# A delta-rule attention with two expert layers: state copies split by PSUM bank, the last output stored by token groups

## The chip, the core and the metric

The kernel runs on one core of a Trainium2 chip. Its engines are TensorE (PE in the profile, with its weight loads as PEld), VectorE (DVE), ScalarE (ACT), GpSimd (POOL) and the DMA queues, which SP and ACT issue to. The metric is the device time of one execution in microseconds; 3 runs give a median.

## What is computed

Three stages follow each other. The first is a delta-rule recurrence over 768 time steps for 4 batches and 8 heads of width 48; the other two are dense layers over the 3072 tokens that it gives, 384 to 2048 to 384.

```python
for t in range(S):                                    # S = 768
    y[:, :, t] = einsum('bhd,bhde->bhe', q[:, :, t], state)
    v_old = einsum('bhde,bhd->bhe', state, k_n[:, :, t])
    state = state + beta_t * einsum('bhd,bhe->bhde', k_n[:, :, t], v_t - v_old)
x = y.transpose(0, 2, 1, 3).reshape(3072, 384)
h = x @ w_in;  x = (h * tanh(softplus(h))) @ w_out            # first layer
h = x @ w2_in; out = (h * clip(h + 3, 0, 6) / 6) @ w2_out     # second layer
```

## The kernel before

The recurrence is computed in 24 chunks of 32 time steps; the four batches lie beside each other on the 128 partitions, 32 each. Each chunk t takes its inner inverse, multiplies the state into its keys (`ksps`), makes its updates `u`, and adds their outer products to the state. The state is the SBUF tile `sbd`. For chunks 0 to 3 the sum over the chunks stays in PSUM, in two banks `dps[0]` and `dps[1]` (in the profile `dsps`): the bank b // 2 holds batch b, on partitions from 64 (b % 2) (`S_part`, line 791). After each of these chunks' matmuls (`S_mm`, L818) `S_copy` (line 795) copies the four batches to `sbd`, two copies a batch: the even batches by DVE (L804), the odd ones by ACT (L801). The next chunk's `ksps` matmuls (L767) need all of them. From chunk 4 on `S_add` (L829) adds on DVE.

The first layer's tokens come in blocks of 512 (6 blocks, each four chunks); it starts as soon as chunk 3's tokens are there, at about 96 us, and runs beside the rest of the recurrence. The second layer starts at about 657 us and runs alone. Each block n of it has 16 steps: `hps` matmuls (L1127), two activations, and 12 matmuls that add to four accumulators `p` (L1285), one for each group s of 128 rows: partition 32 b + t and group s are time step 32 s + t of the block, of batch b. `flush2` (line 1291) copies the four accumulators to the tile `osb`, in turn by ACT (L1300) and DVE (L1298), and then stores the block batch by batch (L1305): a store is 32 rows x 4 groups x 384 numbers, 192 KB. In the last block two of the four stores are issued by ACT, the others by SP.

Nothing is scheduled at run time but the waits. The order of the instructions on each engine is made while the kernel is built, by the class `Flow` (line 28): each part of the work is a generator that asks for an engine and a time, and `Flow` picks the earliest by fixed costs. `warm` (line 1438) fills TensorE with matmuls of no use until the first layer's first step. Two instructions on different engines that read the same PSUM bank get a wait between them.

Of the kernel before, what the change touches and what calls it, by code (L numbers as in the profile page):

```python
# [8 lines left out]
F32 = mybir.dt.float32  # L9
# [3 lines left out]
ACTF = mybir.ActivationFunctionType  # L13
# [3 lines left out]
C = 32  # L17
# [109 lines left out]
def tile_delta_rule__moe_mish__moe_hardswish(  # L127
# [12 lines left out]
    nc = tc.nc  # L140
    B, H, S, D = q.shape
    NT, DM = out.shape
# [8 lines left out]
    NB = NS // 4  # L151
# [12 lines left out]
    flow = Flow()  # L164

    with tc.manual_schedule():
# [18 lines left out]
        sbd = ap_.tile([128, B, NP, 2 * D], F32, name="sbd")  # L185
# [20 lines left out]
        def room(*keys):  # L206

            first = keys[0][0] in "KUS"  # L210

            def test():
                x = sorted((bank_at[b], b) for b in usable if bank_at[b] is not None)
                others = len(keys) + sum(k[0] != "H" for k in held)
                fits = len(x) >= len(keys) + (0 if first else sum(chain))
                if len(usable) < 8 and keys[0][0] != "H" and others >= len(usable):
                    fits = False
                if first:
                    chain[:] = [] if fits or len(usable) == 8 else [len(keys)]
                if not fits:  # L220
                    return None
                x = x[:len(keys)]
                for key, (_, b) in zip(keys, x):
                    bank_at[b], held[key] = None, b
                return x[-1][0]
            return test
# [5 lines left out]
        def release(key):  # L232
            bank_at[held.pop(key)] = flow.cur
# [557 lines left out]
        def S_part(b, r):  # L791

            return dps[b // 2][64 * (b % 2):64 * (b % 2) + D, r]

        def S_copy(t, b):

            for r in range(2):
                o = sbd[64 * r:64 * r + D, b, :, D * r:D * (r + 1)]
                if b % 2:
                    yield "ACT", 0.33, 0  # L800
                    nc.scalar.activation(out=o, in_=S_part(b, r), func=ACTF.Copy)  # L801
                else:
                    yield "DVE", 0.35, 0
                    nc.vector.tensor_copy(out=o, in_=S_part(b, r))  # L804
            if t == 3 and b % 2:
                release(("S", b // 2))
            flow.set(f"sbd{t}.{b}")

        def S_mm(t):

            if t == 0 or t >= 4:
                for half in range(2):
                    dps[half] = bank(("S", half), [128, 2, NP, D], "dsps")
            for r in range(2):
                for j in range(NP):
                    for b in range(B):
                        p = slice(C * b, C * (b + 1))
                        nc.tensor.matmul(  # L818
                            out=S_part(b, r)[:, j, :],
                            lhsT=kp(t)[p, j, r, 0:D], rhs=ut[t][p, 2 * j + r, :],  # L820
                            start=(t == 0 or t >= 4) and j == r == 0, stop=True, skip_group_check=True,
                        )
            flow.set(f"S{t}")
# [10 lines left out]
        def rec():  # L834


            for t in range(NS):
# [8 lines left out]
                if t:  # L846
# [18 lines left out]
                    if tg:  # L865
# [4 lines left out]
                    r = ap_.tile([128, H, D], F32, tag="r", name="r")  # L870
                    nc.vector.tensor_tensor(
                        out=r.rearrange("p h d -> p (h d)"), in0=vt.pop(t).rearrange("p h d -> p (h d)"),
# [4 lines left out]
                else:  # L877
                    r = vt.pop(t)
# [28 lines left out]
                if 0 < t < 4:  # L907
                    u = gp.tile([128, 512], F32, tag="ghi", name="u")[:, 0:H * D].rearrange("p (h d) -> p h d", h=H)
                else:
                    u = ap_.tile([128, H, D], F32, tag="u", name="u")  # L910
# [6 lines left out]
                if t < 4:  # L917
                    if t == 0:
                        yield room(("S", 0), ("S", 1))
                    yield "PE", 0.8, None, 64  # L920
                    S_mm(t)
                    flow.add(mu(t), pen=0.02)
                    for b in range(B):
                        flow.add(S_copy(t, b))
                    continue
                yield f"mt{t}"
                if not last:
# [15 lines left out]
        def mu(t):  # L943
            yield f"mt{t}"
            yield "PE", 0.85, None, 64
            MU_pe(t)
            yield from finish_y(t)
# [148 lines left out]
        xhl, acc = {}, {}  # L1096
# [104 lines left out]
        def moe():  # L1201
# [34 lines left out]
            while done < 2 * NB * KF - 1:  # L1236
                done += 1
                yield from mm2_second(done)
# [31 lines left out]
        def mm2_second(u):  # L1270
            n, f = divmod(u, KF)
            g, e = divmod(f, 4)
            yield f"lo2.{7 * g + KD + e}"
            yield f"g{u}"
            if f == 0:
                yield f"flush{n - 1}"
            yield "PE", 12 * 0.178, 0
            if f == 0:
                acc[n] = [(ps_o if s < 3 else ps_b).tile([128, DM], F32, tag=f"o{s}", name=f"p{s}") for s in range(4)]
            hi, lo = gs.pop(u)  # L1280
            wh, wl = wo[2, g]
            for s in range(4):
                c = slice(128 * s, 128 * (s + 1))
                for x, (a, w) in enumerate(((hi, wh), (hi, wl), (lo, wh))):
                    nc.tensor.matmul(out=acc[n][s], lhsT=a[:, c], rhs=w[:, e, :],  # L1285
                                     start=(f == 0 and x == 0), stop=(f == KF - 1 and x == 2))
            flow.set(f"mm2.{u}")
            if f == KF - 1:
                flow.add(flush2(n), pen=-0.2)

        def flush2(n):
            a, i = acc.pop(n), n - NB
            yield "lo2.27"
            o = p2.tile([128, 4, DM], F32, tag=f"r{i % 3}", name="osb")
            for s in range(4):
                yield ("DVE", 0.45) if s % 2 else ("ACT", 0.5)
                if s % 2:
                    nc.vector.tensor_copy(out=o[:, s, :], in_=a[s])  # L1298
                else:
                    nc.scalar.activation(out=o[:, s, :], in_=a[s], func=ACTF.Copy)  # L1300
            flow.set(f"flush{n}")
            yield "SP", 0.3
            for b in range(B):
                r0 = b * S + 128 * i
                (nc.scalar if i == NB - 1 and b % 2 else nc.sync).dma_start(  # L1305
                    out=out[r0:r0 + 128, :].rearrange("(t s) d -> s t d", s=C),
                    in_=o[C * b:C * (b + 1)],
                )
            if i == NB - 1:
                flow.set("end")  # L1310

        def phase2():

# [30 lines left out]
        p2 = ps_b = None  # L1344
# [112 lines left out]
        flow.add(matrices(), pen=lambda: 0.0 if "D0" not in flow.ev else 0.3)  # L1457
        flow.add(quads(0), pen=-0.1)
        flow.add(rec(), margin=busy(0.0, 0.8))
        flow.add(scale_v(), pen=busy(0.6, 0.0))  # L1460
        flow.add(loads_start())
# [51 lines left out]
```

## Time and profile before

| | us |
|---|---|
| median of 3 runs | 1069.98 |
| lowest, highest | 1068.26, 1071.07 |
| the profiled execution | 1064.65 |
| its span in the profile | 1062.9 |
| TensorE busy | 1030.7 |
| DVE, ACT, POOL busy | 644.8, 453.5, 224.0 |

The profiled execution is one run of the same program; the times in the rows below count from the start of its span. A row of the instructions in order gives start and duration, and in brackets how long the engine had been idle and which instruction released it; "issue" stands where the profile shows nothing that was waited for. q1 is SP's DMA queue and q10 ACT's. TensorE's granted clock is given as a share of its higher level.

### The profile page before, as it was taken

How to read it: one execution, taken by the hardware profiler on the slowest of the kernel's cores; microseconds unless marked ns; L12 is line 12 of the kernel's file. 1: busy time of each engine (PE TensorE's matmuls, PEld its weight loads, DVE VectorE, ACT ScalarE, POOL GpSimd, SP SyncE). 2: the span in 40 equal slices, each digit the busy share in tenths (PEclk: the TensorE clock that was granted, in tenths of full speed). 3: DMA queues.
4: the chain of work that ended last, by engine and by line, in shares of the span. 5: the costliest groups of instructions: out<-in, count | busy, mean ns of one | idle time of the engine just before them, and what ended most of it. 6: DMA issues, size and time to landing. Idle time of an engine off the chain costs nothing.

```text
span 1062.9 us, 30634 instructions
## 1 busy us (share of the span) xinstructions
PE 1030.7 (97%) x13252; PEld 853.9 (80%) x13252; DVE 644.8 (61%) x1460; ACT 453.5 (43%) x916; POOL 224.0 (21%) x240
## 2 busy tenths in 40 slices
PE   8889998999989999999999999999999999999997
PEld 5556776787868777787778787999999999999996
DVE  6777958968577586958833899734343343433432
ACT  4455545544443444445324556433342332432432
POOL 3403223342433524243322332000000000000000
PEclk9999998999989999999999999999999999999999
DMA  5753244332432424232212544202010020110101
GB/s 95 164 141 78 82 100 124 70 72 40 74 75 53 81 41 87 40 67 39 60 22 76 179 123 146 74 1 60 1 32 29 1 60 1 25 36 1 31 1 30
DMA packets 149063, 66.64 MB, mean 63 GB/s; under 512 B 133024, under 2 KB 136096, under 8 KB 148928
## 3 DMA queue, kind: packets, MB, share of 16 engines
q1 hardware_dynamic: 146432, 63.84, 25.1%
q8 instruction: 104, 1.70, 0.7%
q10 hardware_dynamic: 2496, 0.84, 0.4%
q14 instruction: 31, 0.25, 0.1%
HBM read 51.02 MB, written 13.63 MB: 61 GB/s over the span
## 4 chain that ended last, share of the span: by engine, by line
PE 51%; DVE 21%; issue 3%; DMA 2%; ACT 1%; SPq 1%; POOL 1%; DVEq 0%; POOLq 0%; ACTq 0%
PE hps L1127 24%; PE p L1285 19%; DVE tmp L725 7%; DVE tp L732 6%; PE o L1148 5%; DVE sbd L829 3%; DMA ash<-ad 2%; DVE cw L1072 1%; DVE cw L1069 1%; DVE xl L1109 1%; POOL nn L399 1%; PE ksps L767 1%; SPq L737 1%; DVE nn L401 1%; DVE cw L1066 0%
## 5 line engine op out<-in xcount | busy, mean ns | idle before, releaser
L1127 PE MATMUL hps<-xl,wih 128*128 128x512 f32 x576 | 228.2, 396 | 4.0 <-DVE xl L1109 3.9
L1127 PE MATMUL hps<-xh,wih 128*128 128x512 f32 x576 | 228.9, 397 | 0.4 <-ACT xh L1105 0.4
L1127 PE MATMUL hps<-xh,wil 128*128 128x512 f32 x576 | 227.0, 394 | 0.0
L1167 POOL TENSOR_TENSOR glo<-g,ghi 128x512 fp32r<-128x512 f32 x96 | 129.5, 1349 | 271.4 <-ACT ghi L1133 210.7
L1260 DVE SCALAR_TENSOR_TENSOR r<-r,hps 128x512 f32<-128x512 f32 x96 | 66.0, 688 | 166.6 <-ACT r L1258 166.6
L1258 ACT ACTIVATE r<-hps,half_c 128x512 f32<-128x512 f32 x96 | 66.1, 689 | 174.4 <-PE hps L1127 174.4
L725 DVE TENSOR_TENSOR tmp<-tp,ash 128x126 f32<-128x126 f32 (+22 forms) x248 | 101.9, 411 | 52.9 <-DMA ash<-ad 46.2
L1127 PEld LDWEIGHTS hps<-xl,wih 128*128 128x128 f32 x576 | 108.6, 189 | 27.4 <-DVE xl L1109 8.2
L1285 PE MATMUL p<-woh,glo 128*128 128x384 f32 x384 | 129.5, 337 | 0.0
L1285 PE MATMUL p<-woh,ghi 128*128 128x384 f32 x384 | 129.2, 337 | 0.0
L1285 PE MATMUL p<-wol,ghi 128*128 128x384 f32 x384 | 128.9, 336 | 0.0
L1127 PEld LDWEIGHTS hps<-xh,wil 128*128 128x128 f32 x576 | 108.6, 189 | 22.8
L1127 PEld LDWEIGHTS hps<-xh,wih 128*128 128x128 f32 x576 | 108.6, 189 | 21.8 <-ACT xh L1105 1.0
L1158 ACT ACTIVATE g<-hps 128x512 f32<-128x512 f32 x96 | 57.2, 596 | 153.2 <-PE hps L1127 149.5
L1148 PE MATMUL o<-ghi,wol 128*128 128x512 f32 x288 | 114.1, 396 | 0.0
L1148 PE MATMUL o<-ghi,woh 128*128 128x512 f32 x288 | 113.9, 395 | 0.0
L1266 DVE TENSOR_TENSOR glo<-r,ghi 128x512 fp32r<-128x512 f32 x96 | 66.5, 693 | 58.7 <-ACT ghi L1133 58.2
L1133 ACT ACTIVATE ghi<-r 128x512 fp32r<-128x512 f32 x96 | 60.7, 632 | 67.3 <-DVE r L1260 67.3
L732 DVE TENSOR_TENSOR tp<-tp,tmp 128x126 f32<-128x126 f32 (+22 forms) x248 | 81.5, 329 | 7.4
L1148 PE MATMUL o<-glo,woh 128*128 128x512 f32 x288 | 83.6, 392 | 0.0
L1285 PEld LDWEIGHTS p<-woh,ghi 128*128 128x128 f32 x384 | 72.2, 188 | 4.0
L1285 PEld LDWEIGHTS p<-wol,ghi 128*128 128x128 f32 x384 | 72.1, 188 | 3.9
(140 smaller groups left out, 1404.7 us busy)
## 6 DMA issues: line engine op xcount, KB each, us to landing
raw<-in_moe_w_in_dram SPq DMA_DIRECT2D x24, 512.0 KB, 3.6
raw<-in_moe_w_out_dram SPq DMA_DIRECT2D x32, 384.0 KB, 3.2
vt<-in_v_dram SPq DMA_DIRECT2D x96, 48.0 KB, 2.5
x2d<-x2out SPq DMA_DIRECT2D x6, 768.0 KB, 4.2
x2in<-x2d SPq DMA_DIRECT2D x6, 768.0 KB, 6.1
kpad<-in_k_dram SPq DMA_DIRECT2D x88, 48.0 KB, 2.1
qpad<-in_q_dram SPq DMA_DIRECT2D x88, 48.0 KB, 2.2
out_dram<-osb SPq DMA_DIRECT2D x22, 192.0 KB, 3.3
```

Of the source, the lines that this page charges most:

```text
L725: nc.vector.tensor_tensor(out=tv, in0=x[:, 0:m, j:j + 1].to_broadcast([128, m, n]), in1=a[:, j + 1:C, j:j + 1].rearrange("p i o -> p o i") ...
L732: nc.vector.tensor_tensor(out=x[:, 0:m, j + 1:C], in0=x[:, 0:m, j + 1:C], in1=tv, op=ALU.add)
L829: nc.vector.tensor_tensor(out=o, in0=o, in1=S_part(b, r), op=ALU.add)
L1127: nc.tensor.matmul(out=ps[0], lhsT=w[:, kk, c], rhs=xhl[n][xi][:, kk, :], start=(kk == 0 and x == 0), stop=(kk == KD - 1 and x == 2))
L1133: nc.scalar.activation(out=hi, in_=g, func=ACTF.Copy)
L1148: nc.tensor.matmul(out=acc[i][dc], lhsT=w[:, e, 128 * dc:128 * (dc + 1)], rhs=a, start=(f == 0 and x == 0), stop=(f == KF - 1 and x == 2))
L1158: nc.scalar.activation(out=g, in_=ps, func=ACTF.Mish)
L1167: nc.gpsimd.tensor_tensor(out=lo, in0=g, in1=hi.bitcast(F32), op=ALU.subtract)
L1258: nc.scalar.activation(out=r, in_=ps, func=ACTF.Relu, scale=1.0 / 6.0, bias=half_c)
L1260: nc.vector.scalar_tensor_tensor(out=r, in0=r, scalar=1.0, in1=ps, op0=ALU.min, op1=ALU.mult)
L1266: nc.vector.tensor_tensor(out=lo, in0=r, in1=hi.bitcast(F32), op=ALU.subtract)
L1285: nc.tensor.matmul(out=acc[n][s], lhsT=a[:, c], rhs=w[:, e, :], start=(f == 0 and x == 0), stop=(f == KF - 1 and x == 2))
```

## The change

Two parts. `S_copy` takes a bank (`half`) in place of a batch: the four copies of bank 0 are done by DVE and those of bank 1 by ACT. And the last block of the second layer gets a flush of its own, `last_out`: each of the groups 0 to 2 is stored by SP as soon as it is copied, one store for all four batches; group 3 is copied in two halves of 64 partitions, by DVE and ACT, and stored in two halves, by SP and ACT. The other blocks' stores are as before, all on SP.

```diff
--- before.py
+++ after.py
@@ -792,19 +792,20 @@
 
             return dps[b // 2][64 * (b % 2):64 * (b % 2) + D, r]
 
-        def S_copy(t, b):
-
-            for r in range(2):
-                o = sbd[64 * r:64 * r + D, b, :, D * r:D * (r + 1)]
-                if b % 2:
-                    yield "ACT", 0.33, 0
-                    nc.scalar.activation(out=o, in_=S_part(b, r), func=ACTF.Copy)
-                else:
-                    yield "DVE", 0.35, 0
-                    nc.vector.tensor_copy(out=o, in_=S_part(b, r))
-            if t == 3 and b % 2:
-                release(("S", b // 2))
-            flow.set(f"sbd{t}.{b}")
+        def S_copy(t, half):
+
+            for b in (2 * half, 2 * half + 1):
+                for r in range(2):
+                    o = sbd[64 * r:64 * r + D, b, :, D * r:D * (r + 1)]
+                    if half:
+                        yield "ACT", 0.33, 0
+                        nc.scalar.activation(out=o, in_=S_part(b, r), func=ACTF.Copy)
+                    else:
+                        yield "DVE", 0.35, 0
+                        nc.vector.tensor_copy(out=o, in_=S_part(b, r))
+                flow.set(f"sbd{t}.{b}")
+            if t == 3:
+                release(("S", half))
 
         def S_mm(t):
 
@@ -920,8 +921,8 @@
                     yield "PE", 0.8, None, 64
                     S_mm(t)
                     flow.add(mu(t), pen=0.02)
-                    for b in range(B):
-                        flow.add(S_copy(t, b))
+                    for half in range(2):
+                        flow.add(S_copy(t, half))
                     continue
                 yield f"mt{t}"
                 if not last:
@@ -1286,7 +1287,7 @@
                                      start=(f == 0 and x == 0), stop=(f == KF - 1 and x == 2))
             flow.set(f"mm2.{u}")
             if f == KF - 1:
-                flow.add(flush2(n), pen=-0.2)
+                flow.add((flush2 if n < 2 * NB - 1 else last_out)(n), pen=-0.2)
 
         def flush2(n):
             a, i = acc.pop(n), n - NB
@@ -1302,12 +1303,32 @@
             yield "SP", 0.3
             for b in range(B):
                 r0 = b * S + 128 * i
-                (nc.scalar if i == NB - 1 and b % 2 else nc.sync).dma_start(
+                nc.sync.dma_start(
                     out=out[r0:r0 + 128, :].rearrange("(t s) d -> s t d", s=C),
                     in_=o[C * b:C * (b + 1)],
                 )
-            if i == NB - 1:
-                flow.set("end")
+
+        def last_out(n):
+            a, i = acc.pop(n), n - NB
+            o = p2.tile([128, 4, DM], F32, tag=f"r{i % 3}", name="osb")
+            rows = out.rearrange("(b u) d -> b u d", b=B)
+            for s in range(4):
+                c = slice(128 * i + C * s, 128 * i + C * (s + 1))
+                if s < 3:
+                    yield ("DVE", 0.45) if s % 2 else ("ACT", 0.5)
+                    if s % 2:
+                        nc.vector.tensor_copy(out=o[:, s, :], in_=a[s])
+                    else:
+                        nc.scalar.activation(out=o[:, s, :], in_=a[s], func=ACTF.Copy)
+                    yield "SP", 0.3
+                    nc.sync.dma_start(out=rows[:, c, :], in_=o[:, s, :])
+                else:
+                    yield "DVE", 0.45
+                    nc.vector.tensor_copy(out=o[0:64, s, :], in_=a[s][0:64])
+                    nc.scalar.activation(out=o[64:128, s, :], in_=a[s][64:128], func=ACTF.Copy)
+                    nc.sync.dma_start(out=rows[0:2, c, :], in_=o[0:64, s, :])
+                    nc.scalar.dma_start(out=rows[2:4, c, :], in_=o[64:128, s, :])
+            flow.set("end")
 
         def phase2():
```

The first place in the built program is the copies after chunk 0 on ACT. The numbers behind the names are the tiles': `dsps_1296` is bank 0, `dsps_1297` bank 1. Before:

```order
L1061 ACTIVATE cv_1331<-raw_849 128x384 [waits DMAHW4_49,DVE_49]
L801 ACTIVATE sbd_109<-dsps_1296 48x4x48 [waits PE_49]
L801 ACTIVATE sbd_109<-dsps_1296 48x4x48 [waits DVE_49]
L801 ACTIVATE sbd_109<-dsps_1297 48x4x48 [waits PE_49]
L801 ACTIVATE sbd_109<-dsps_1297 48x4x48 [waits DVE_49]
L956 ACTIVATE y_1403<-yps_1007 128x384 [waits PE_49]
```

and after:

```order
L1090 ACTIVATE wih0_1151<-cv_1195 128x512 [waits DVE_49]
L1062 ACTIVATE cv_1331<-raw_849 128x384 [waits DMAHW4_49,DVE_49]
L802 ACTIVATE sbd_109<-dsps_1297 48x4x48 [waits PE_49]
L802 ACTIVATE sbd_109<-dsps_1297 48x4x48 x3
L957 ACTIVATE y_1403<-yps_1007 128x384 [waits PE_49]
```

The copies keep their place in ACT's order; they now read one bank and wait for TensorE alone. On DVE it is the same with bank 0.

The second place is the end of the program on SP. `osb` is the copied output; the shape is that of the side in memory. Before, the last two blocks:

```order
L1305 DMA out_0_dram<-osb_13219 32x4x384 [waits DMAHW4_49,DVE_49,Activation_49]
L1305 DMA out_0_dram<-osb_13219 32x4x384 [waits DMAHW5_49]
L1305 DMA out_0_dram<-osb_13219 32x4x384
L1305 DMA out_0_dram<-osb_13219 32x4x384 [waits DMAHW7_49]
L1305 DMA out_0_dram<-osb_13684 32x4x384 [waits DMAHW1_49,DVE_49,Activation_49]
L1305 DMA out_0_dram<-osb_13684 32x4x384 [waits DMAHW3_49]
```

and after:

```order
L1306 DMA out_0_dram<-osb_13220 32x4x384 [waits DMAHW7_49]
L1324 DMA out_0_dram<-osb_13685 4x32x384 [waits DMAHW0_49,Activation_49]
L1324 DMA out_0_dram<-osb_13685 4x32x384 [waits DMAHW1_49,DVE_49]
L1324 DMA out_0_dram<-osb_13685 4x32x384 [waits DMAHW2_49,Activation_49]
L1329 DMA out_0_dram<-osb_13685 2x32x384 [waits DMAHW3_49,DVE_49]
```

Each of SP's last stores now waits for one copy, and its side in memory begins with the batches; the SBUF side is 128 partitions (64 for a half).

The third place is the end of the program on ACT. Before:

```order
L1258 ACTIVATE r2_13641<-hps_13630,half_c_96 128x512 [waits PE_49,Activation_49]
L1133 ACTIVATE ghi_13656<-r2_13641 128x512 [waits DVE_49]
L1300 ACTIVATE osb_13684<-p0_13259 128x384 [waits DMAHW4_49,DMAHW5_49,DMAHW2_49,PE_49]
L1300 ACTIVATE osb_13684<-p2_13261 128x384 [waits PE_49]
L1305 DMA out_0_dram<-osb_13684 32x4x384 [waits DMAHW0_49,DVE_49,Activation_49]
L1305 DMA out_0_dram<-osb_13684 32x4x384 [waits DMAHW2_49]
```

and after:

```order
L1134 ACTIVATE ghi_13657<-r2_13642 128x512 [waits DVE_49]
L1322 ACTIVATE osb_13685<-p0_13260 128x384 [waits DMAHW4_49,DMAHW5_49,DMAHW2_49,PE_49]
L1322 ACTIVATE osb_13685<-p2_13262 128x384 [waits PE_49]
L1328 ACTIVATE osb_13685<-p3_13263 64x384 [waits DVE_49]
L1330 DMA out_0_dram<-osb_13685 2x32x384 [waits DMAHW4_49,Activation_49]
```

ACT now also copies half of the last accumulator, after DVE's half of the same bank, and issues one store in place of two. Between these places the orders of PE, DVE and ACT differ only between about 92 and 125 us of the profile before, where the first layer starts; PE has one `warm` matmul more there.

## Rows read from the trace of the kernel before

**Rows 1.** The page, part 1: an engine's busy us, share of the span, instructions.

```profile
PE 1030.7 (97%) x13252; PEld 853.9 (80%) x13252; DVE 644.8 (61%) x1460; ACT 453.5 (43%) x916; POOL 224.0 (21%) x240
```

**Rows 2.** By stretches: busy us of each engine, PEclk, DMA share, GB/s.

```profile
96.00:125.00 29.00, 29.00 (x483) 23.19 (x483) 27.23 (x62) 14.70 (x31) 10.79 (x9) 1.00 0.29 81
657.00:1057.00 400.00, 399.33 (x2007) 362.00 (x2005) 161.94 (x254) 145.59 (x234) 0.00 (x0) 1.00 0.10 28
```

**Rows 3.** Tile sbd, 0 to 140 us: ns min/median/max; under them who waited: us, times.

```profile
L801 ACT ACTIVATE sbd<-dsps x16: 326/327/328, 57.6 to 88.8; 48x192 f32<-48x192 f32 x16
L804 DVE COPY sbd<-dsps x16: 350/350/352, 58.0 to 89.2; 48x192 f32<-48x192 f32 x16
...
  ACT sbd L801: 6.2, 8
  DVE sbd L804: 3.6, 7
```

**Rows 4.** The instructions in order: start us, us; in brackets idle us and releaser. Chunk 1.

```profile
66.75 0.35 DVE L804 COPY sbd<-dsps 48x192 f32<-48x192 f32 x1 [0.45 <-PE dsps L818]
...
69.00 0.33 ACT L801 ACTIVATE sbd<-dsps 48x192 f32<-48x192 f32 x1 [0.42 <-DVE sbd L804]
...
69.38 0.63 PEld L767 LDWEIGHTS ksps<-sbd,kqt 128*32 128x32 f32 x26 [0.22 <-ACT sbd L801]
```

**Rows 5.** The same, PE: a filler group, and two waits in chunks 1 and 2.

```profile
58.62 1.25 PE L1444 MATMUL warm<-late 128*128 128x512 bf16 x5
...
71.15 0.27 PE L419 MATMUL tps<-ident,qpad 128*128 128x128 f32 x1 [0.22 <-issue]
...
76.17 0.66 PE L818 MATMUL dsps<-u,kpad 32*48 32x48 f32 x40 [1.13 <-issue]
```

**Rows 6.** The same, DVE, chunk 5.

```profile
156.11 2.97 DVE L829 TENSOR_TENSOR sbd<-sbd,dsps 48x192 f32<-48x192 f32 x8 [4.61 <-PE dsps L818]
```

**Rows 7.** The same, PE, waiting for chunk 6's additions; then two stretches behind it.

```profile
174.56 0.33 PE L767 MATMUL ksps<-sbd,kqt 128*32 128x96 f32 x2 [2.14 <-DVE sbd L829]
...
176.00:180.00 4.00, 3.77 (x95) 2.74 (x95) 2.65 (x5) 1.01 (x2) 0.00 (x0) 0.50 0.75 173
180.00:184.00 4.00, 4.00 (x24) 3.17 (x13) 3.67 (x14) 1.34 (x4) 0.73 (x1) 0.68 0.23 84
```

**Rows 8.** The instructions in order, the last output.

```profile
1054.81 0.49 ACT L1300 ACTIVATE osb<-p 128x384 f32<-128x384 f32 x1 [2.57 <-PE p L1285]
...
1056.37 0.56 DVE L1298 COPY osb<-p 128x384 f32<-128x384 f32 x1 [0.49 <-PE p L1285]
1057.00 0.79 SPq L1305 DMA_DIRECT2D out_dram<-osb  x2
1057.01 0.86 ACTq L1305 DMA_DIRECT2D out_dram<-osb  x2
```

**Rows 9.** DMA, 1050 to 1063 us: GB/s in 40 slices; a queue's packets, MB.

```profile
GB/s 0 0 0 0 0 0 0 0 0 0 0 0 0 0 0 0 0 0 0 0 0 0 0 0 203 184 198 189 189 165 222 321 279 251 180 38 0 0 0 0
...
q10 hardware_dynamic: 288, 0.39, 12.8%
```

**Rows 10.** DMA, 205 to 210 us; then three rows of the whole span.

```profile
q1 hardware_dynamic: 1088, 0.20, 22.1%
...
vt<-in_v_dram SPq DMA_DIRECT2D x4, 48.0 KB, 2.2
...
q10 hardware_dynamic: 2496, 0.84, 0.4%
...
kpad<-in_k_dram ACTq DMA_DIRECT2D x8, 48.0 KB, 2.5
...
bst<-in_beta_dram ACTq DMA_DIRECT2D x2, 24.0 KB
```

**Rows 11.** DMA, 212.5 to 219 us: GB/s in 40 slices; then the issue on SP.

```profile
GB/s 143 144 59 0 0 0 0 0 63 340 353 391 403 378 391 391 391 378 391 365 353 202 13 13 25 101 0 0 0 0 0 0 0 0 0 0 0 0 0 0
...
212.68 0.60 SPq L1180 DMA_DIRECT2D x2d<-x2out  x1
```

## The prediction

> **What bounds the kernel now.** I read the busy shares first: TensorE is busy for 97% of the span [rows 1]. Then the table by stretches: from 96 us, where the first expert layer starts, TensorE has no gap to 125 us, and in the second layer it is busy 399.33 of 400 us [rows 2]. So a microsecond saved on another engine reaches the end only where TensorE waits for that engine, or before TensorE starts, or after it has stopped. The change touches two such places: the state copies of chunks 0 to 3 (57 to 90 us), and the last 6 us, where TensorE has finished and the result is only copied and stored. The working is made against the profiled execution, 1064.65 us with a span of 1062.9; the median of the three runs is 1069.98, and I put the difference onto that. A difference under 0.3% (3.2 us) is about what a measurement of this kernel can't tell from no change.
>
> **The copies.** Each of the four chunks has 8 copies, 4 on VectorE (350 ns each) and 4 on ScalarE (327 ns), and the two engines take turns: ScalarE idled 6.2 us for VectorE's copies and VectorE 3.6 us for ScalarE's [rows 3]. In chunk 1 they run from 66.75 to 69.33 [rows 4]. With a bank for each engine that is 4 x 0.37 = 1.5 us, about 1.1 us less. What of it is on the path? TensorE itself waited for a copy once, 0.22 us at 69.38 in chunk 1 [rows 4]. Its next instructions show waits marked "issue", for nothing that the profile names: 0.22 us at 71.15 and 1.13 us at 76.17 [rows 5]. I take these as the moments at which its next instructions arrive, so an earlier start makes the wait longer and gains nothing. In chunks 0 and 3 the second bank is complete only after such a wait, so ScalarE ends where it did; in chunk 2 ScalarE is free sooner, but its weight copy after the next instruction still waits for VectorE. TensorE's order up to the start of the first layer is the same row for row, its filler matmuls included. I take 0; bounds 0 and -1.1 us (chunk 1's gain comes through whole).
>
> What is left is that VectorE is free some 1.1 us earlier after the last of the four chunks, too. The order of TensorE, VectorE and ScalarE changes between 92 and 125 us and is then the same again to the last output. VectorE's lead does not last: later it stands idle for TensorE, 4.61 us at 156.11 [rows 6]. TensorE gets one filler matmul (`warm`) more ahead of the first layer: five take 1.25 us [rows 5], so +0.2 us. Between 96 and 125 us TensorE had no gap to lose [rows 2]; a new one there, if VectorE's new order is late, I bound by the one 1.13 us wait above. Sum so far +0.2 us, between -0.9 and +1.3.
>
> **The last output.** Before: four copies, the last from 1056.37 to 1056.93, then four stores of 192 KB, two on SP and two on ScalarE's queue, issued from 1057.00 to 1057.87 [rows 8]; bytes flow from about 1057.8 to 1061.5, at 165 to 321 GB/s [rows 9], and the span ends at 1062.9. After: the store of token group 0 is issued when its copy ends, 1054.81 + 0.49 = 1055.30 [rows 8], groups 1 and 2 half a microsecond after each other, and group 3 in two halves. The second half gains nothing from being on two engines: its copy on ScalarE waits for VectorE's, since both read one bank, so it ends at about 1057.5, later than 1056.93. That would be covered by the three stores under way.
>
> What decides is how fast the new stores run. A store before has 32 outermost entries on both sides (32 token rows x 4 x 384). A store after has 128 rows on the SBUF side but 4 (the batches) outermost in memory, and each half has 2. The trace tells how many DMA engines a transfer uses by its completion packets. Four loads of v, 32 x 8 rows each, are 1088 packets = 4 x (256 + 16) [rows 10]: 16 completions each. Two stores are 288 packets = 2 x (128 + 16) [rows 9]. ScalarE's queue carried 2496 packets in all [rows 10]: 8 loads of k are 8 x 272 = 2176, two stores 288, and 32 remain for two loads of beta with 8 rows each, 16 apiece: 8 rows and 8 completions. So a transfer with 8 outermost entries was spread over 8 engines, though its rows of 3 KB could have been cut further: an outermost entry is not divided. By that a store with 4 outermost entries uses 4 engines and a half with 2 uses 2. No row shows a transfer whose two sides differ below 16, so whether the smaller side decides is my inference, and its opposite is the first rival.
>
> The Trainium skill, DMA: Bandwidth & Descriptors, section "Why a DMA increments its semaphore by 16 and not by 1", has the piece that no row shows: the count is the largest number up to 16 that divides the outermost sizes of both sides, and the lowest-numbered engines are taken. The beta loads' 8 agree; by this page it is 4 and 2, on one set of engines, and the page speaks against this change.
>
> Now the sum. If all stores lie on the same lowest engines (no row shows them moving about; the other choice belongs to the first rival), the busiest engine carries 128 / 4 = 32 rows from each of three stores and 64 / 2 = 32 from each half: 160 rows of 1536 bytes, where each engine carried 32 before. A row costs: at most what it cost before, 3.7 us / 32 = 0.117 us [rows 9]; at least what one engine does in the x2d stores, 391 GB/s / 16 = 24.4 GB/s [rows 11], 0.063 us. The fastest stretch of the old stores, 321 GB/s [rows 9], is 20 GB/s or 0.077 us per row, so 0.117 was not the engine's own limit. With 4 engines alone I take 0.075. Issue at 1055.37, first bytes 0.8 us later as before (1057.00 to 1057.8), and 0.2 more since a store with unlike sides takes longer to issue (0.60 us [rows 11] against 0.79 for two [rows 8]): 1056.4. 160 x 0.075 = 12.0, so the last byte lands at 1068.4 in place of 1061.4: +7.0 us. With 0.063 it is 10.1 and +5.1, with 0.117 it is 18.7 and +13.7.
>
> Forecast: +7.0 + 0.2 = +7.2 us, 1071.85 on the profiled execution and **1077.2** on the median.
>
> **Rivals.** First, not slower: the stores do spread over 16 engines, because the SBUF side with its 128 rows decides, or each store takes other engines. Then the same 786 KB flow without a gap from 1056.4 and need 3.7 us: 1060.1 in place of 1061.4, -1.3, and with the filler -1.1: 1068.9, no change that can be told. For it: the old stores were spread so, and the first is issued 1.63 us earlier. Against it: the beta loads' 8. It decides at the point where the first store's completions are counted: 16 or 4.
>
> Second: few engines, and each at the old 0.117 us per row: +13.9, 1083.9. For it: it is the price of this very row size. Against it: the 321 GB/s stretch.
>
> Third: VectorE's 1.1 us last until 174.56, where TensorE waits 2.14 us for its state additions and then runs at half the granted clock (0.50 from 176 to 180, the lower level, and 0.68 to 184; it had been waiting) [rows 7]. If that stall went with its clock loss, 2.1 + 4 x 0.50 + 4 x 0.32 = 5.4 us, the sum is +1.8: 1071.8. For it: the stall is VectorE's lateness. Against it: the 4.61 us that VectorE waits for TensorE between [rows 6].
>
> **How the numbers follow.** Forecast 0.68; second rival 0.12; first 0.12; third with the forecast's tail 0.05; first and third together, 1069.98 - 1.1 - 5.4 = 1063.5, 0.03. Slower by over 0.3%: 0.68 + 0.12 = 0.80. Within 0.3%: 0.12 + 0.05 = 0.17. Faster: 0.03. The range leaves out the first and third rival, 0.20. Its low end is the price of 0.063 per row (1069.98 + 5.1 + 0.2 = 1075.3) less 0.9 for chunk 1's gain and 1.4 for the spread of the runs; its high end the second rival's 1083.9 plus 1.1 for a new gap: 1073 to 1085.
>
> **What would show it.** In the profile after: the last stores' packets, 128 rows and 4 completions for one of groups 0 to 2, 64 and 2 for a half; the mean busy share of the DMA engines at a quarter or less after 1056 us, and bytes until about 1068; the span's end some 7 us later relative to the last matmul, which itself ends within 1 us of 1056.3. ScalarE's and VectorE's copies of a chunk run side by side with no wait between them, and TensorE's "issue" waits in chunks 1 and 2 are longer. I am wrong if those stores write 16 completions each, if the bytes are through by 1062, or if the last matmul ends more than 2 us from where it did.

## The result and the profile after

The changed kernel is slower: 1074.22 us median beside 1068.24 of before (six runs each), a ratio of 1.0056 with a 95% interval of 1.0036 to 1.0076, that is 3.8 to 8.1 us. The forecast was +7.2 us and "slower"; the time lies in the range of 1073 to 1085.

Where the time went is read from two places of the profiled execution (1073.29 us, span 1071.6). First the copies: the part of the tile `sbd` in the first 100 us of after (ns min/median/max, and who waited), which answers to [rows 3].

```profile
L805 DVE COPY sbd<-dsps x16: 350/354/361, 58.7 to 88.6; 48x192 f32<-48x192 f32 x16
L802 ACT ACTIVATE sbd<-dsps x16: 322/326/328, 58.8 to 89.6; 48x192 f32<-48x192 f32 x16
its engine sat idle before it (us, times) until:
  PE dsps L819: 8.3, 8
...
who waited for it (us, times):
```

Nobody waits for a copy any more; the 6.2 and 3.6 us in which the two engines waited for each other are gone. And yet TensorE's next product with the state does not start earlier. TensorE's own rows of chunk 1 in the kernel before:

```profile
66.27 0.47 PE L818 MATMUL dsps<-u,kpad 32*48 32x48 f32 x19 [0.20 <-issue]
...
68.99 1.23 PE L767 MATMUL ksps<-sbd,kqt 128*32 128x96 f32 x32
```

and the instructions of chunk 1 in order in after, which answer to [rows 4, 5]:

```profile
66.93 0.47 PE L819 MATMUL dsps<-u,kpad 32*48 32x48 f32 x19 [0.74 <-issue]
...
67.41 1.48 DVE L805 COPY sbd<-dsps 48x192 f32<-48x192 f32 x4 [0.99 <-PE dsps L819]
67.49 1.35 ACT L802 ACTIVATE sbd<-dsps 48x192 f32<-48x192 f32 x4 [0.52 <-PE dsps L819]
...
69.65 0.87 PE L767 MATMUL ksps<-sbd,kqt 128*32 128x96 f32 x32 [0.25 <-PE yps L787]
...
72.09 0.27 PE L419 MATMUL tps<-ident,qpad 128*128 128x128 f32 x1 [1.09 <-issue]
```

The copies now take 1.5 us side by side and are through at 68.9. The `ksps` matmuls start at 69.65 behind TensorE's own `yps`, 2.72 us after the last `S_mm` matmuls started; before, that distance was 2.72 us too (66.27 to 68.99). TensorE spends that time on other work, and it covers the copies. Of the old ones a little stuck out: `ksps` took 1.23 us, with its wait for a copy, and takes 0.87 now. The wait marked "issue" behind them is 1.09 us here and was 0.22, but it is no measure of the copies: with the same new copies it is 0.27 us in e4_whole and e5_halves and absent in e1_copies, and with the old ones it is absent in e2_last_out.

Second the tail. Before, the last matmul was this one:

```profile
1056.00 0.34 PE L1285 MATMUL p<-woh,glo 128*128 128x384 f32 x1
```

Here are the instructions at the end of after, beside [rows 8]: the last matmul, and the issues of the stores.

```profile
1056.04 1.96 SPq L1324 DMA_DIRECT2D out_dram<-osb  x3
...
1056.71 0.34 PE L1286 MATMUL p<-woh,glo 128*128 128x384 f32 x1
...
1058.10 1.08 SPq L1329 DMA_DIRECT2D out_dram<-osb  x1
1058.19 0.64 ACTq L1330 DMA_DIRECT2D out_dram<-osb  x1
```

And the DMA from 1056 us to the end of the span, in 40 slices of 0.39 us (busy share of the 16 engines in tenths, GB/s), beside [rows 9]:

```profile
DMA  0001221222232222402122211111111111110000
GB/s 0 0 0 32 20 16 51 71 95 95 98 102 87 102 102 95 67 4 32 32 71 95 91 67 59 43 51 51 47 51 51 47 51 51 47 39 4 0 0 0
DMA packets 528, 0.79 MB, mean 50 GB/s; under 512 B 16, under 2 KB 528, under 8 KB 528
```

Bytes flow from 1057.2 to about 1070.2, after a slow start at 100 GB/s, then at 50; before they needed 3.7 us. The 16 packets under 512 bytes are the completions of all five stores, 3 x 4 + 2 x 2 of them, where the four stores of before had 4 x 16. A quarter and then an eighth of the engines is busy. From the start of the last matmul to the end of the span there are 14.9 us, in place of 1062.9 - 1056.00 = 6.9.

That distance, called the tail below, is the number to compare. The whole time moves by several us from run to run of one and the same kernel (before lay between 1065.07 and 1072.75 us in its runs beside the experiments), while the tail does not: it was 6.9 to 7.0 us in all five profiles with the old last output. With the change's last output it is less steady: the two profiles, of after and of e2_last_out, have 14.9 and 14.1 us.

### The profile page after: what moved, and what is told of

Read it like the earlier page. It is cut to its first block, busy times and chain, and to the rows that moved or that the text cites. A ratio compares the mean times of both kernels' runs of the same rounds, so it can differ in the third digit from the quotient of the medians.

```text
span 1071.6 us, 30611 instructions
## 1 busy us (share of the span) xinstructions
PE 1027.6 (96%) x13223; PEld 856.2 (80%) x13253; DVE 645.2 (60%) x1460; ACT 454.9 (42%) x917; POOL 225.6 (21%) x240
## 4 chain that ended last, share of the span: by engine, by line
PE 54%; DVE 19%; issue 2%; DMA 2%; ACT 1%; SPq 1%; POOL 1%; DVEq 0%; POOLq 0%; ACTq 0%
PE hps L1128 25%; PE p L1286 19%; PE o L1149 6%; DVE tmp L725 6%; DVE tp L732 5%; DVE sbd L830 3%; DMA ash<-ad 2%; DVE cw L1073 1%; DVE cw L1070 1%; PE ksps L767 1%; POOL nn L399 1%; DVE xl L1110 1%; PE ups L777 1%; PE yps L787 1%; SPq L737 1%
```

## The experiments

Tails, and ratios to the kernel before on the same chip with their 95% intervals:

| kernel | tail, us | ratio to before |
|---|---|---|
| before | 6.9 | 1 |
| after | 14.9 | 1.0056 (1.0036 to 1.0076) |
| e1_copies | 6.9 | 1.0004 (0.9985 to 1.0024) |
| e2_last_out | 14.1 | 1.0076 (1.0052 to 1.0099) |
| e3_sixteen | 6.2 | 0.9987 (0.9972 to 1.0001) |
| e4_whole | 11.5 | 1.0042 (1.0024 to 1.0060) |
| e5_halves | 19.0 | 1.0117 (1.0102 to 1.0132) |
| e6_one_engine | 7.0 | 0.9947 (0.9931 to 0.9963) |
| e7_spread_partitions | 6.0 | 0.9998 (0.9988 to 1.0009) |
| e8_interleaved | 4.7 | 0.9986 (0.9975 to 0.9997) |
| e9_order_of_e1 | 6.9 | 1.0036 (1.0019 to 1.0054) |
| e10_order_of_e6 | 6.9 | 0.9953 (0.9939 to 0.9967) |
| e11_e6_e8 | 4.7 | 0.9913 (0.9898 to 0.9928) |

### The two parts apart

e1_copies has the change of `S_copy` and the old `flush2`; e2_last_out has `last_out` and the old `S_copy`.

> Only the state copies are changed (one bank for VectorE, one for ScalarE); the last block is stored as before. My theory: the copies are covered by TensorE's other waits, so the median is that of before within 0.3% (0.2 us more for the filler matmul); the tail, from the start of the last matmul to the end of the span, stays at 6.9 us, and the last matmul starts between 1054.5 and 1057.5. Rival: the copies do reach the end. The profile of after shows 8.0 us lost in the tail and the medians only 6.0 us, so the copies would have to give back about 2 us: a median of about 1066 beside 1068.2.

> Only the last output is changed; the state copies are as before. My theory: all of the loss is here. Tail 14.9 us in place of 6.9, and the median 6 to 8 us above before (1074 to 1076). Rival (the copies give back 2 us): also a tail of 14.9, but a median 8 us above before, 2 us above after.

e1_copies: 1068.39 us beside 1068.68. e2_last_out: 1076.01. All of the loss is in the last output, and the copies give back nothing that can be told (the interval of e1_copies is -1.6 to +2.6 us). The 2 us between after's tail and its medians I take for the runs' own spread: in e2_last_out tail (+7.2) and ratio (+8.1 us) differ by half of that, the other way round. Two expectations were missed: the tail of e2_last_out is 14.1 and not 14.9, and the last matmul of e1_copies starts at 1060.85, not between 1054.5 and 1057.5, in an execution of 1069.50 us where that of before had 1064.65.

### How many engines a store gets

e4_whole and e5_halves change the number of outermost entries and nothing else: group 3 whole, or all four groups in halves.

```diff
-                if s < 3:
+                if s < 4:
```

```diff
-                    nc.sync.dma_start(out=rows[:, c, :], in_=o[:, s, :])
+                    nc.sync.dma_start(out=rows[0:2, c, :], in_=o[0:64, s, :])
+                    nc.sync.dma_start(out=rows[2:4, c, :], in_=o[64:128, s, :])
```

> The change with group 3 copied by VectorE at once and stored by one store, as the other groups are, in place of two halves. My theory (four engines for a store, all on the same four, 0.065 us a row): the busiest engine carries 128 rows in place of 160, 32 x 0.065 = 2.1 us less: tail 12.8 us in place of 14.9, with no stretch at 50 GB/s at the end; 516 plus 12 = 528 packets, 16 completions. Rival (the rate is set by how the rows lie in memory, four batches at a time, not by the engines): the same bytes at the same rate, tail 14.9 or, with the copy of one engine, more.

> The change with all four groups stored in two halves of 64 partitions (2 outermost entries in memory) instead of group 3 alone: the same bytes, as early, in eight stores. My theory (2 engines for a half, always the same two, 0.065 us a row): each of two engines carries 256 rows in place of 160: 96 x 0.065 = 6.2 us more, tail 21 us (20 to 22) in place of 14.9; about 50 GB/s from the first byte to the last; 16 completions. Rival (each half takes other engines, and what slows the tail of after is something else): the tail stays at 15 or falls.

GB/s of e4_whole from 1058 to 1070.2 us (slices of 0.31 us), with its packets:

```profile
GB/s 0 0 0 0 45 15 15 40 50 71 91 96 101 101 101 91 101 96 101 96 96 96 91 81 101 101 101 101 101 81 96 101 101 71 50 5 0 0 0 0
DMA packets 528, 0.79 MB, mean 64 GB/s; under 512 B 16, under 2 KB 528, under 8 KB 528
```

and of e5_halves from 1056 to 1078 us (slices of 0.55 us), and within it the queues' packets from 1064 to 1070:

```profile
GB/s 0 0 0 0 0 0 14 17 22 31 31 42 50 36 50 50 50 50 50 50 50 50 50 50 50 50 50 50 50 50 47 50 50 50 50 50 50 34 0 0
...
q1 hardware_dynamic: 136, 0.20, 9.0%
q10 hardware_dynamic: 66, 0.10, 4.4%
```

Once the bytes flow evenly, the rate is 100 GB/s with four outermost entries and 50 with two, whichever queue issues: 25 GB/s for an engine. The halves on ACT's queue do not add engines of their own; in e5_halves both queues together take 9.0 + 4.4 = 13.4% of the time of 16 engines, about two of them. So all stores lie on the same few engines. A row costs 6 us x 2 / 196 = 0.061 us there (202 packets, 6 of them completions), and 3 us x 4 / 187 = 0.064 in after from 1059 to 1062:

```profile
DMA packets 191, 0.29 MB, mean 96 GB/s; under 512 B 4, under 2 KB 191, under 8 KB 191
...
q1 hardware_dynamic: 191, 0.29, 26.1%
```

The tails came out 1.3 and 2.0 us shorter than I expected, and 19.0 lies outside the 20 to 22 that I gave: I had worked from after's tail, and after has a hole, which is to be seen in its GB/s (67, 4, 32, 32 from 1062.2 on, about 1 us lost). ACT's half begins there: from 1059 to 1062 there is no packet of q10. The kernels with stores of one kind have no such hole, and e2_last_out, with the same stores as after, has a shallower one (its tail is 0.8 us shorter). What makes the hole was not tried, and the rest of the 1.3 and 2.0 us is open. All of them start slowly, at a fraction of the rate for the first 1.5 us or more.

### The same early stores with all engines

e3_sixteen issues as early as the change, but stores by batch: groups 0 to 2 when the third is copied, group 3 at the end.

```diff
+                if s >= 2:
+                    g = slice(0, 3) if s == 2 else slice(3, 4)
+                    for b in range(B):
+                        r0 = b * S + 128 * i
+                        (nc.scalar if b % 2 else nc.sync).dma_start(
+                            out=out[r0:r0 + 128, :].rearrange("(t s) d -> s t d", s=C)[:, g, :],
+                            in_=o[C * b:C * (b + 1), g, :],
+                        )
```

> The change with other last stores: when groups 0 to 2 are copied, four stores by batch (32 rows x 3 groups), and when group 3 is copied, four more by batch (32 rows x 1 group), on SP and ACT in turn. As early as the change's, but each has 32 outermost entries on both sides. My theory (the number of engines is the smaller outermost count): 640 packets in the tail, 512 rows and 128 completions, 16 for each store; the DMA share above 0.8 while bytes flow; tail 5.4 to 6.4 us, 0.5 to 1.5 under before. Rival (an early store, or one of small pieces, is slow in itself because it collides with the copies and the last matmuls): tail at least 10 us.

From 1050 to 1072 us (slices of 0.55 us):

```profile
GB/s 0 0 0 0 0 0 0 0 0 0 0 0 0 0 42 212 182 207 296 235 257 0 0 0 0 0 0 0 0 0 0 0 0 0 0 0 0 0 0 0
DMA packets 640, 0.79 MB, mean 36 GB/s; under 512 B 128, under 2 KB 640, under 8 KB 640
```

128 completions for eight stores, 16 each, and a tail of 6.2 us. Storing early is worth 0.7 us; it does no harm in itself.

e8_interleaved keeps the change's idea, one store for a group, and mends its shape: the last block's input is read in another order, so that partition 4 t + b of an accumulator holds step t of batch b, and the side in memory begins with 32 steps.

```diff
+                if n == 2 * NB - 1:
+                    sk = sk.rearrange("p (s b t) -> p s t b", b=B, t=C)
+                    xs = [v.rearrange("p (s t b) -> p s t b", b=B, t=C) for v in xs]
...
-            rows = out.rearrange("(b u) d -> b u d", b=B)
+            rows = out.rearrange("(b u) d -> u b d", b=B)
```

> The change with the last block's tokens in another order: its input is read so that partition 4 t + b (not 32 b + t) of an accumulator is time step t of batch b. A group is then stored by one store with 32 outermost entries in memory and 128 rows in SBUF, four stores on SP, each issued as soon as its group is copied; the copies are not halved. My theory (what is wrong with the change is only its 4 and 2 outermost entries): 16 completions for each store, 512 + 64 = 576 packets, at 300 GB/s or more; the last store is issued as its copy ends, about 0.95 us after the last matmul's start; bytes 0.8 us later, 0.6 us long, and 1.4 us to the end: tail 3.8 to 5.0 us in place of 6.9, 1.9 to 3.1 under before; a time of 1065 to 1067. Rival (storing by groups, four batches at a time, is slow in itself): tail above 10. Second rival (the strided reads of ScalarE and VectorE make the last block late): the last matmul later by more than 3 us.

From 1062 to 1066.7 us (slices of 0.12 us; the last matmul starts at 1062.05):

```profile
GB/s 0 0 0 0 0 183 366 353 405 314 66 261 418 392 353 223 118 366 392 366 314 131 275 392 392 314 275 26 0 0 0 0 0 0 0 0 0 0 0 0
DMA packets 576, 0.79 MB, mean 167 GB/s; under 512 B 64, under 2 KB 576, under 8 KB 576
```

Four stores, 16 completions each, four humps of up to 418 GB/s: each group is almost gone before the next one flows. The tail is 4.7 us, 10.2 shorter than after's with the same state copies and the same bytes, and 6.9 shorter than that of e4_whole, which has the same four stores and unhalved copies too. Together with the step from four entries to two in e5_halves this settles the cause: it is the outermost size.

The second rival's sign, a last matmul later by more than 3 us, is there by the letter (1062.05, before 1056.00), but the profiled execution was the slowest of the twelve (1068.45 us; median 1065.05), and in e11_e6_e8 below the same reads leave the last matmul at 1051.63, no later than the 1053.23 of e6_one_engine.

### Why the old stores started at half their rate

In [rows 9] the old stores flow at 165 to 203 GB/s first and at 321 later. e7_spread_partitions lets store b read every fourth partition in place of 32 neighbours:

```diff
-                    in_=o[C * b:C * (b + 1)],
+                    in_=o[b:128:4] if i == NB - 1 else o[C * b:C * (b + 1)],
```

> The copies of the change; the last block stored by four stores as before, but store b reads partitions b, b + 4, b + 8, ... instead of 32 neighbours, so rows of the last block land in wrong places (the shapes, sizes, queues and the places in memory as a whole are those of before). Before, a row takes about 0.11 us while one store alone is under way and 0.065 where two mix. Theory (16 engines that all read the same 32 partitions get in each other's way): with the partitions spread, 0.065 from the start, 786 KB in 2.1 to 2.6 us in place of 3.7, tail 5.4 to 6.0 in place of 6.9. Rival (the first stores are slow for a reason on the memory side, or because a stream starts slowly): GB/s and tail as before, 6.7 to 7.1.

Two answers for DMA: e1_copies from 1062 to 1067.8 us (old stores), then e7_spread_partitions from 1062 to 1067.7, in slices of 0.14 us.

```profile
GB/s 0 0 0 0 74 222 191 180 201 201 233 180 170 180 191 180 159 191 159 276 318 328 265 275 286 223 276 180 191 96 0 0 0 0 0 0 0 0 0 0
```

```profile
GB/s 0 0 0 0 0 0 0 0 0 0 0 0 0 32 334 356 366 345 367 377 377 356 388 356 366 345 367 388 324 76 0 0 0 0 0 0 0 0 0 0
```

The first theory holds: 334 GB/s from the start and 2.2 us for all bytes. Only 0.9 us of it reaches the tail (6.0): two such stores take 1.34 us to issue on SP in place of 0.79 [rows 8], and the bytes start later.

### The copies' own price, and an order that was faster

e6_one_engine was meant to make the copies worse: all eight by VectorE.

```diff
-                    if half:
+                    if half > 1:
```

> The state copies of both banks by VectorE, eight in a row, ScalarE none; the last output as before. Each chunk's copies then end about 1.45 us later than with an engine for each bank. My theory (the copies are off the path, by a cover of the order of 1 to 2 us in each chunk): at most 1.5 us above e1_copies, no change that can be told from before (1066 to 1071). Rival (the copies are on the path of all four chunks, and e1_copies showed nothing since its gain was lost elsewhere): 4 x 1.45 = 5.8 us above, 1074.

Neither: 1060.83 us beside 1067.07, faster by 0.5%. The planner (`Flow`) had booked other engines and made another order. e9_order_of_e1 and e10_order_of_e6 take the two apart: the first runs the copies on VectorE but books them as e1_copies does, the second runs them on two engines but books them as e6_one_engine does. TensorE's order is that of their model in each.

```diff
 e9_order_of_e1
                         yield "ACT", 0.33, 0
-                        nc.scalar.activation(out=o, in_=S_part(b, r), func=ACTF.Copy)
+                        nc.vector.tensor_copy(out=o, in_=S_part(b, r))
 e10_order_of_e6
-                        yield "ACT", 0.33, 0
+                        yield "DVE", 0.35, 0
```

> All eight copies of a chunk by VectorE, as in e6_one_engine, but booked by the planner as in e1_copies (four of them on ScalarE), so that TensorE's order is that of e1_copies row for row. It tells the copies' own cost from the order that their booking leads to. My theory (e6_one_engine was 5.7 us faster because the planner made another order, in which the stall with a half clock at 300 to 312 us is gone; the copies themselves are covered): the time of before or up to 1.5 us more, 1067 to 1070, and the stall of 300 to 312 us is there again, granted clock under 0.8 in the stretch around it. Rival (copies on one engine are in themselves better, for instance since ScalarE's weight copies come sooner): 1060.8, as e6_one_engine.

> One bank copied by VectorE and one by ScalarE, as the change does it, but booked by the planner as eight copies on VectorE, so that TensorE's order is that of e6_one_engine row for row. My theory (the order is what gained, the copies' place does not matter): 1060.8 within 2 us, granted clock 1.00 from 296 to 312 us. Rival (the gain is from the copies being on one engine): 1066 to 1069 as before and e1_copies.

The gain goes with the order: 0.9947 and 0.9953 with the one, 1.0004 and 1.0036 with the other. Two stretches of e1_copies, then of e6_one_engine (TensorE's busy us, granted clock, DMA share, GB/s):

```profile
172.00:190.00 18.00, 14.80 (x351) 0.81 0.54 118
296.00:316.00 20.00, 16.43 (x361) 0.79 0.29 50
```

```profile
172.00:190.00 18.00, 12.67 (x241) 0.81 0.46 121
296.00:316.00 20.00, 18.54 (x256) 1.00 0.30 66
```

In the new order TensorE waits less between 296 and 316 us, and its clock stays at the higher level: 2.1 us of gaps and 20 x 0.21 = 4.2 us of clock, less 2.1 us lost in a longer wait at 178 to 183. That makes 4.2 us, a rough estimate, since it counts the clock in the gaps too. The last matmuls of these two executions are 7.6 us apart (1060.85 and 1053.23); where the rest lies was not settled. The stall itself goes with the order in every profile: from 296 to 316 us TensorE is busy 15.9 to 16.6 us at a granted clock of 0.74 to 0.83 in the ten kernels with the old order, e9_order_of_e1 among them (16.56 at 0.75), and 18.5 us at 1.00 in the three with the new one.

In the same order the later copies cost 0.0032 of 1067 us, 3.4 us, more than the 1.5 I expected and less than 5.8 (the two intervals overlap a little). The rows of e9_order_of_e1 name waits of TensorE that e1_copies does not have, or has shorter (0.49 us in place of 1.98 at the third):

```profile
61.55 0.86 PE L767 MATMUL ksps<-sbd,kqt 128*32 128x96 f32 x30 [0.39 <-DVE sbd L805]
...
73.60 0.55 PE L964 MATMUL xps<-ident,y 128*128 128x128 f32 x3 [0.69 <-DVE r L872]
...
85.09 0.55 PE L964 MATMUL xps<-ident,y 128*128 128x128 f32 x3 [1.98 <-ACT kqt L425]
```

The copies do not end 1.45 us later in each chunk of e9_order_of_e1, as in e6_one_engine: counted from a chunk's first copy they end about 1.1, 1.1, 2.1 and 0.6 us later than in e1_copies, some 4.8 us in all. So in this order the cover of the copies ends close to where the copies ended before: copying sooner gains nothing that can be told, and copying later costs about 3.4 us of the 4.8. In the order of e6_one_engine this was not shown. There ScalarE, whose work had been booked to VectorE, came to its four copies in pieces, and in e10_order_of_e6 a chunk's copies end 3.0 to 3.9 us after the first one starts, in place of 3.0; that cost nothing that can be told (0.9953 and 0.9947), and sooner copies were not tried in that order.

e11_e6_e8 puts the faster order and the mended last output together.

> The eight copies on VectorE of e6_one_engine together with the interleaved last output of e8_interleaved. If the two gains lie in different places they add: tail 4.65 us, 2.2 us less than e6_one_engine, 1058.5 (1057 to 1060). Rival (the order that e6_one_engine was given is sensitive, and the changed emission of the last block's input moves the stall back in): 1065, as e8_interleaved.

1058.11 us beside 1067.36, 0.9913: the two gains add, and this version beats both kernels by 0.9% and more.

## Why the prediction was right

**The copies at nothing: right in the sum, but not shown by the reason that I gave.** e1_copies shows no change that can be told. That ScalarE and VectorE work side by side with no wait was seen as said. But I had let the "issue" waits take up the gain, and said that they would grow in chunks 1 and 2. In chunk 2 the wait is shorter in after (0.58 us for 1.13), and as short with the old copies in e2_last_out (0.58); in chunk 1 it goes from none to 1.36 us (e1_copies, e8_interleaved) among kernels with the same copies. What the rows do show in chunk 1 is TensorE's own work: 2.72 us from the last `S_mm` matmuls to `ksps`, with the old copies as with the new. So only the wait inside `ksps`, 0.36 us, was there to be gained, and the prediction's other sentence, that TensorE waited for a copy just once, would have been enough. What covers the copies in the other chunks was only measured as a whole, by e1_copies and e9_order_of_e1. The one filler matmul more (0.2 us) is too small to be told.

**VectorE's lead is lost: right.** It waits for TensorE as before, and the stall that the third rival counted on is there:

```profile
157.50 2.60 DVE L830 TENSOR_TENSOR sbd<-sbd,dsps 48x192 f32<-48x192 f32 x7 [4.76 <-PE dsps L819]
```

```profile
175.96 0.32 PE L767 MATMUL ksps<-sbd,kqt 128*32 128x96 f32 x2 [1.98 <-DVE sbd L830]
```

The rival's kind of price was no fancy, though: e6_one_engine removed such a stall with its loss of clock at another place.

**Four and two engines, always the same: right.** The step that I had called an inference was shown by after's 16 completions and by e4_whole, e5_halves and e8_interleaved. By this count the Trainium skill, DMA: Bandwidth & Descriptors, section "Why a DMA increments its semaphore by 16 and not by 1", agrees with the trace. With it the first rival (all 16 engines) falls, and the second (0.117 us a row) by the rates of 100 and 50 GB/s.

**The term of the rows: 12.0 us forecast, 13.0 measured, from parts that were off in opposite ways.** A row costs 0.061 to 0.064 us, my lower bound, not 0.075: I had taken 0.075 from the old stores' best stretch, and e7_spread_partitions shows that these were slowed by their partitions. 160 x 0.063 = 10.1. What I had not counted is the slow first 1.5 us and the hole of about 1 us where the halves come in. That 12.0 lies so near to 13.0 is therefore in part luck: a row priced too high stood in for two losses that I did not know of. So the tail lost 8.0 us in place of 7.0 (7.2 in e2_last_out), and the last bytes came at 1070.2 and not 1068.4, of which 0.7 is the later last matmul.

**The second half of group 3:** its copy ended at 1058.2, 1.45 us after the last matmul's start, where the single copy of before ended 0.93 after it, as said; it lay behind the other stores.

**The median:** 3.0 us under the forecast. 1.7 of them are the median of before, 1068.24 in six runs and 1069.98 in the three that I had; 1.2 are the effect, which the interval does not tell from 7.2.

## What to carry to other kernels

Before a store is cut or merged, look at the outermost size on both sides: here 4 in memory meant 4 engines and 100 GB/s whatever stood on the other side, and changing the order of the rows, so that the outermost size was 32, turned the same idea from +8 us into -2.2 in the tail. Waits of engines for each other say little about the end as long as the busiest engine has work of its own there (here TensorE's 2.72 us); the cover can be measured by making the copies later on purpose, with the order held fixed. Where a planner makes the order, an edit that books other engines is two edits, and only a kernel that books one way and runs the other tells them apart.

## What the runs showed of the hardware

Sixteen engines that read the same 32 neighbouring partitions moved 160 to 230 GB/s; the same stores over 32 partitions four apart moved 334 to 388 (e7_spread_partitions). The Trainium skill, SBUF — State Buffer, section "Door 1: The DMA port swizzle (why [64,N] ≈ [32,N])", says that 32 neighbouring partitions reach only half of the memory's 16 ports; the factor of two agrees.

Stores with few engines start slowly: 12 to 52 GB/s for about 1.5 us, in after, e2_last_out, e4_whole and e5_halves alike, while e8_interleaved is at 366 GB/s in its second slice of 0.12 us. What delays them was not tried.
